# Reordering the first row group's second-layer products, two weight casts and three inverse roots

## The chip, the cores and the metric

The kernel runs on one core of one Trainium2 chip. The metric is the device time of one execution in microseconds (us). Three timed runs of the kernel before took 400.53, 398.08 and 399.92 us, median 399.92 us. Below, TensorE (PE) is the matrix engine, VectorE (DVE) and ScalarE (ACT) are the two elementwise engines that read its results, GpSimd (POOL) is the third elementwise engine, and SyncE (SP) issues the transfers.

## The reference

Each of 2048 rows of 512 numbers is normalised. The result is the input, plus a spectral filter of the normalised rows (a two-dimensional transform, a product with weights, the inverse transform), plus a two-layer network of the normalised rows:

```python
xn = _layernorm(x, axis=-1)              # x is 1 x 2048 x 512
X = rfft2(xn) * (w_r + 1j * w_i)         # spectral branch
y = irfft2(X, s=(S, D))
h = xn @ w1 + b1                         # w1 is 512 x 1792
act = h * tanh(softplus(h))              # "Mish"
return x + y + act @ w2                  # w2 is 1792 x 512
```

## The kernel before

Every product is made from 16-bit halves: a number is split into a high half (its 16-bit rounding) and a low half (what is left), and a product is three matmuls, high by high, high by low, low by high. The helper `mm3` (lines 85 to 92) issues these three for one output tile: line 88 takes both high halves, line 91 the high half of the stationary operand and the low half of the moving one, line 92 the reverse.

The 2048 rows are cut into four row groups of 512 (g = 0 to 3), and each into four blocks of 128 (s = 0 to 3). For each row group the network has 14 column tiles (f = 0 to 13). `mlp_up` makes one 128 x 512 tile of the first layer (12 matmuls, line 781, result `ph`); ScalarE applies Mish (line 795, tile `hb`) and makes its high half (line 813, tile `a`), VectorE the low half (line 816). `mlp_down(g, f, a)` adds the tile's part of the second layer into four accumulators `pa_0` to `pa_3`, one for each block of rows: 12 matmuls. Its moving operand is the weight `w2`, kept in seven pieces of two column tiles each, so tiles f = 2c and 2c + 1 read piece c. A piece is split by `hi_w2` on ScalarE (line 496) and `lo_w2` on VectorE (line 499); piece 0 is split earlier, by lines 379 and 380. Both halves lie in the tensor `w2r`.

After a start in which x, `w1` and `w2` are loaded and the first eleven up tiles are made, the program is written out in 26 slots, and within them PE, ACT, DVE and POOL keep the order in which the code is written (`in_order`). Each slot holds one up or down tile, and beside it pieces of the preparation of the later row groups: statistics of the rows (`sums_`, lines 209 and 211), the factors of the normalisation (`factors`, line 217 and on), the normalisation itself (`norm`: ScalarE lines 233 and 236, POOL line 237, tile `xh`), its transposition (`turned_rows`: PE line 242 into `pt`, then copies into `xnT` by VectorE line 333 and ScalarE line 334), and the first step of the spectral transform (`s1_forward`: PE into `psS`; ScalarE line 123 and VectorE lines 127 and 128 in `butterfly`, tiles `bc` and `bt`; ScalarE line 132 and POOL line 133 make `y`, which a transfer writes to memory). A piece of `w2` given to slot k is cast by ScalarE at the end of slot k and by VectorE in slot k + 1:

```python
for c in range(1, 7):
    at[(0, 3, 6, 8, 11, 14)[c - 1]]["w2"].append(c)
```

`factors` needs the inverse square root of a variance, 128 x 4 numbers for each row group. It is worked out by a bit trick and two polynomial steps. For row group 0 this is `rsqrt_of`, eight instructions on VectorE (lines 161 to 176) and a ninth for `nb`. For row groups 1 to 3 it is `rsqrt_plain`, eleven instructions on POOL (lines 187 to 197) and two for `nb` (lines 222 and 223).

The result tiles rotate through few buffers: `ph` and `pt` share two, the transform's `psS` and its successors two, `bt` two. A matmul into a tile waits until the tile two turns earlier has been read. After the slots come the rest of the spectral branch, with the up and down tiles of row groups 1 to 3 spread between its steps, and the outputs.

Of the kernel before, what the change touches and what calls it, by code (L numbers as in the profile page):

```python
# [12 lines left out]
F32 = mybir.dt.float32  # L13
I32 = mybir.dt.int32
AF = mybir.ActivationFunctionType
ALU = mybir.AluOpType
# [3 lines left out]
P = 128  # L20
# [21 lines left out]
def spectral_mlp_kernel(ctx, tc, x, wt, w0, w1, b1, w2, cT, cIT, cM, out):  # L42
    nc = tc.nc
# [3 lines left out]
    sp = ctx.enter_context(tc.tile_pool(name="sp", bufs=1))  # L47
# [38 lines left out]
    def mm3(ps, stat, mov, start, stop, order=False):  # L86

        first = nc.tensor.matmul(ps, stat(0), mov(0), start=start, stop=False)  # L88
        if order:
            tc.keep_in_program_order(first)  # L90
        nc.tensor.matmul(ps, stat(0), mov(1), start=False, stop=False)  # L91
        return nc.tensor.matmul(ps, stat(1), mov(0), start=False, stop=stop)  # L92
# [63 lines left out]
    def rsqrt_of(g, ve):  # L156

        r = sp.tile([P, 4], F32, tag="rr", name=f"rr_{g}_0", bufs=4)
        v = nc.vector

        v.tensor_scalar(r.bitcast(I32), ve.bitcast(I32), -0.5, float(0x5F3759DF), op0=ALU.mult, op1=ALU.add)
        t = sp.tile([P, 4], F32, tag="rt", name=f"rt_{g}_0", bufs=2)
        v.tensor_mul(t, r, r)
        q = sp.tile([P, 4], F32, tag="rq", name=f"rq_{g}_0", bufs=2)
        v.scalar_tensor_tensor(q, t, -192.0, ve, op0=ALU.mult, op1=ALU.mult)
        n = sp.tile([P, 4], F32, tag="rr", name=f"rr_{g}_1", bufs=4)
        v.scalar_tensor_tensor(n, q, 576.0, r, op0=ALU.add, op1=ALU.mult)

        t = sp.tile([P, 4], F32, tag="rt", name=f"rt_{g}_1", bufs=2)
        v.tensor_mul(t, n, n)  # L170
        w = sp.tile([P, 4], F32, tag="rq", name=f"rq_{g}_1", bufs=2)
        v.scalar_tensor_tensor(w, t, 384.0**-2, ve, op0=ALU.mult, op1=ALU.mult)
        p = sp.tile([P, 4], F32, tag="rt", name=f"rt_{g}_2", bufs=2)
        v.scalar_tensor_tensor(p, w, -10.0 / 3, w, op0=ALU.add, op1=ALU.mult)
        rs = sp.tile([P, 4], F32, tag="rs", name=f"rs_{g}", bufs=2)
        v.scalar_tensor_tensor(rs, p, 5.0, n, op0=ALU.add, op1=ALU.mult)
        return rs

    def rsqrt_plain(g, ve):


        def tile_(name):
            return sp.tile([P, 4], F32, tag=f"g{name}", name=f"g{name}_{g}", bufs=2)

        v = nc.gpsimd
        r, t, q, n, w, u, rs = (tile_(k) for k in ("r", "t", "q", "n", "w", "u", "s"))
        v.tensor_scalar(r.bitcast(I32), ve.bitcast(I32), -0.5, float(0x5F3759DF), op0=ALU.mult, op1=ALU.add)
        v.tensor_mul(t, r, r)
        v.tensor_mul(q, t, ve)
        v.tensor_scalar(q, q, -192.0, 576.0, op0=ALU.mult, op1=ALU.add)  # L190
        v.tensor_mul(n, q, r)
        v.tensor_mul(t, n, n)
        v.tensor_mul(w, t, ve)
        v.tensor_scalar(u, w, 384.0**-2, -10.0 / 3, op0=ALU.mult, op1=ALU.add)
        v.tensor_mul(u, u, w)
        v.tensor_scalar(u, u, 384.0**-2, 5.0, op0=ALU.mult, op1=ALU.add)
        v.tensor_mul(rs, u, n)
        return rs

    def sums(g, ts, ss):  # L200

        if 0 in ss:
# [11 lines left out]
    def factors(g, mv):  # L214

        ve = sp.tile([P, 4], F32, tag="ve", name=f"ve_{g}", bufs=2)
        nc.vector.tensor_scalar(ve, mv[:, :, 1], 1e-5, None, op0=ALU.add)
        nb = sp.tile([P, 4], F32, tag="nb", name=f"nb_{g}", bufs=2)
        if g:

            rs = rsqrt_plain(g, ve)
            nc.gpsimd.tensor_mul(nb, mv[:, :, 0], rs)
            nc.gpsimd.tensor_scalar(nb, nb, -1.0, None, op0=ALU.mult)
        else:
            rs = rsqrt_of(g, ve)
            nc.vector.scalar_tensor_tensor(nb, mv[:, :, 0], -1.0, rs, op0=ALU.mult, op1=ALU.mult)
        return mv, rs, nb

    def norm(g, s, ts, mr):
# [157 lines left out]
    w2t = w2r.rearrange("p c j d -> p c (j d)").bitcast(F16).rearrange("p c (h j d) -> p c h j d", h=2, j=2)  # L387
# [438 lines left out]
    pacc = {}  # L826

    def mlp_down(g, f, a):
        if f == 0:
            pacc[g] = [ps_a.tile([P, D], F32, tag="a", name=f"pa_{g}_{s}") for s in range(4)]  # L830
        for s in range(4):
            last_mm = mm3(
                pacc[g][s],
                lambda h: a[:, h, s * P : (s + 1) * P],
                lambda h: w2t[:, f // 2, h, f % 2, :],
                f == 0,
                f == NFC - 1,
            )
# [162 lines left out]
    xh, mr, mv = {(0, s): xhs[s] for s in range(4)}, {}, {}  # L1001
    at = {k: {"sums": [], "norm": [], "turn": [], "w2": [], "then": []} for k in range(N_SLOTS)}
# [26 lines left out]
    at[19]["then"].append(matrices)  # L1029
    at[21]["then"].append(load_it)  # L1030
    for c in range(1, 7):
        at[(0, 3, 6, 8, 11, 14)[c - 1]]["w2"].append(c)

    for k in range(N_SLOTS - 10, N_SLOTS):
        at[k]["then"].append(lambda: next(maxima, None))
# [2 lines left out]
    _, hi, lo = last["up"]  # L1038
# [44 lines left out]
    start, used = done[0], 0.0  # L1083
# [8 lines left out]
    start, n = done[0], len(todo)  # L1092
# [187 lines left out]
```

## Time and profile before

| what | before |
|---|---|
| median of three runs | 399.92 us (398.08 to 400.53) |
| the profiled execution's own time | 398.09 us |
| its span, first to last instruction | 396.3 us |
| PE busy | 379.8 us (96%) |
| VectorE busy | 241.2 us (61%) |
| ScalarE busy | 210.3 us (53%) |
| POOL busy | 68.9 us (17%) |
| transfers | 61.61 MB |
| granted PE clock | 1.00 |

A row of the timeline gives the start in us, the duration in us, the engine and the line of the kernel, the operation, the output and inputs by the program's names without their numbers, and the shapes; a bracket holds the idle time of that engine just before, and what released it. Consecutive instructions of an engine overlap a little, so a row's duration is longer than the distance to the next start.

### The profile page before, as it was taken

The page shows a single profiled execution, that of the slowest core. Times are in us where ns is not written, and L with a number is a line of the kernel's source. Part 1 is how long each engine was busy: PE and PEld are TensorE (multiplying, and loading weights), DVE is VectorE, ACT ScalarE, POOL GpSimd, SP SyncE. Part 2 cuts the span into 40 slices and gives each one's busy share as a digit, 9 for nine tenths or more (in the row PEclk, how much of TensorE's full clock was granted, in tenths as well). Part 3 has the DMA queues.
Part 4 walks back from the last instruction along what each step waited for, and adds up shares of the span by engine and source line. Part 5 has one row for each costly group of instructions (what it writes and reads, how often), then busy time and mean ns, then how long its engine had stood idle before and what let it go on. Part 6 is the DMA issues. An engine that isn't in the chain of part 4 may idle for free. (4 is left out here: it accounts for less than half of the span.)

```text
span 396.3 us, 6567 instructions
## 1 busy us (share of the span) xinstructions
PE 379.8 (96%) x2481; PEld 190.7 (48%) x2481; DVE 241.2 (61%) x505; ACT 210.3 (53%) x337; POOL 68.9 (17%) x100
## 2 busy tenths in 40 slices
PE   8799897999999999999999999999999999999995
PEld 3444343455544445456444565454655456444442
DVE  5789773465566724984597644957349972424334
ACT  3869858478665426564644555366455464423110
POOL 0000018366644400000021100121001120220000
PEclk9999999999999999999999999999999999999999
DMA  8995014335157894055732636226652022744556
GB/s 286 372 402 244 1 55 132 108 126 168 53 160 217 237 276 127 0 134 131 242 108 80 163 105 180 91 104 159 216 160 80 27 81 73 218 151 135 172 194 253
DMA packets 49519, 61.61 MB, mean 155 GB/s; under 512 B 3776, under 2 KB 36032, under 8 KB 48848
## 3 DMA queue, kind: packets, MB, share of 16 engines
q1 hardware_dynamic: 49488, 61.20, 49.1%
q8 instruction: 19, 0.31, 0.3%
q14 instruction: 12, 0.10, 0.1%
HBM read 44.38 MB, written 16.78 MB: 154 GB/s over the span
## 5 line engine op out<-in xcount | busy, mean ns | idle before, releaser
L781 PE MATMUL ph<-xnT,w1t 128*128 128x512 f16 x672 | 153.4, 379 | 1.3 <-ACT xnT L334 0.8
L781 PEld LDWEIGHTS <-w1t 128*128 128x128 f16 x672 | 65.0, 98 | 78.6 <-issue 1.5
L91 PE MATMUL pa<-w2r,a 128*128 128x512 f16 x224 | 84.9, 379 | 2.9 <-DVE w2r L499 1.9
L88 PE MATMUL pa<-w2r,a 128*128 128x512 f16 x224 | 85.0, 379 | 0.8 <-ACT w2r L496 0.5
L92 PE MATMUL pa<-w2r,a 128*128 128x512 f16 x224 | 84.9, 379 | 0.0
L795 ACT ACTIVATE hb<-ph,b1t,sc_exp 128x512 f32<-128x512 f32 x56 | 43.2, 772 | 56.1 <-PE ph L781 56.0
L816 DVE SCALAR_TENSOR_TENSOR a<-hb,sc_a,a 128x512 f16<-128x512 f32 x56 | 41.8, 750 | 51.0 <-ACT a L813 50.7
L133 POOL TENSOR_TENSOR tt<-bt_t,tt 128x512 f16<-128x512 f32 x16 | 19.9, 1245 | 186.3 <-ACT tt L132 186.3
L813 ACT ACTIVATE a<-hb,sc_a 128x512 f16<-128x512 f32 x56 | 40.1, 720 | 1.5
L92 PEld LDWEIGHTS <-a 128*128 128x128 f16 x224 | 21.9, 98 | 29.1 <-issue 3.7
L91 PEld LDWEIGHTS <-a 128*128 128x128 f16 x224 | 21.9, 98 | 25.5 <-issue 1.9
L88 PEld LDWEIGHTS <-a 128*128 128x128 f16 x224 | 21.9, 98 | 25.2 <-issue 0.8
L379 ACT ACTIVATE u<-r,sc_u 128x512 f16<-128x512 f32 x16 | 11.5, 720 | 23.6 <-DVE r L679 15.5
L133 POOL TENSOR_TENSOR y<-bt_s,y 128x512 f16<-128x512 f32 x16 | 18.7, 1177 | 10.8 <-issue 6.0
L132 ACT CAST tt<-bt_t 128x512 f16<-128x512 f32 x16 | 9.9, 616 | 15.9 <-DVE bt_t L128 12.5
L906 DVE SCALAR_TENSOR_TENSOR m<-psY,sc_k,m 128x512 f32<-128x512 f32 x12 | 8.7, 746 | 14.9 <-PE psY L92 14.9
L237 POOL TENSOR_TENSOR xh<-xs,xh 128x512 f16<-128x512 f32 x12 | 14.5, 1210 | 10.3 <-ACT xh L236 10.3
L734 DVE SCALAR_TENSOR_TENSOR at<-psA,at 128x512 f16<-128x512 f32 x16 | 10.7, 687 | 8.7 <-ACT at L733 8.7
L611 ACT ACTIVATE ix<-psD 64x512 f32<-64x512 f32 x16 | 9.5, 594 | 11.2 <-PE psD L599 10.9
L132 ACT CAST y<-bt_s 128x512 f16<-128x512 f32 x16 | 9.9, 616 | 10.4 <-DVE bt_s L128 7.6
L588 DVE SCALAR_TENSOR_TENSOR z<-psP,z 128x512 f16<-128x512 f32 x16 | 10.5, 684 | 7.8 <-ACT z L587 7.8
L127 DVE SCALAR_TENSOR_TENSOR bt_s<-psS,bc_s 128x256 f32<-128x256 f32 x16 | 6.7, 422 | 13.1 <-ACT bc_s L123 9.5
(158 smaller groups left out, 512.7 us busy)
## 6 DMA issues: line engine op xcount, KB each, us to landing
wt<-in_wt_dram SPq DMA_DIRECT2D x32, 256.0 KB
x<-in_x_dram SPq DMA_DIRECT2D x8, 512.0 KB
d_y<-y SPq DMA_DIRECT2D x16, 256.0 KB
wm<-in_wt_dram SPq DMA_DIRECT2D x8, 512.0 KB
yt<-d_y SPq DMA_DIRECT2D x16, 256.0 KB
d_a<-at SPq DMA_DIRECT2D x32, 128.0 KB
ai<-d_a SPq DMA_DIRECT2D x16, 256.0 KB
d_t<-tt SPq DMA_DIRECT2D x16, 256.0 KB
```

The source lines that it names most:

```text
L88: first = nc.tensor.matmul(ps, stat(0), mov(0), start=start, stop=False)
L91: nc.tensor.matmul(ps, stat(0), mov(1), start=False, stop=False)
L92: return nc.tensor.matmul(ps, stat(1), mov(0), start=False, stop=stop)
L132: nc.scalar.copy(out[:, :, 0, :], tv)
L133: nc.gpsimd.tensor_sub(out[:, :, 1, :], tv, out[:, :, 0, :])
L237: nc.gpsimd.tensor_sub(xh[:, 1, :], xs, xh[:, 0, :])
L379: hi = nc.scalar.activation(dst_h, src, AF.Copy, scale=scale)
L734: nc.vector.scalar_tensor_tensor(at[:, :, 1, :], psv, 2.0**-15, at[:, :, 0, :], op0=ALU.mult, op1=ALU.subtract)
L781: last_mm = nc.tensor.matmul(ph, w1t[:, hs, dc, f * P : (f + 1) * P], xnT[g][:, hm, dc, :], start=n == 0, stop=n == 11)
L795: nc.scalar.activation(hb, ph, AF.Mish, bias=b1t[:, f : f + 1], scale=s_exp[k])
L813: hi = nc.scalar.activation(a[:, 0, :], hb, AF.Copy, scale=sc["a"])
L816: lo = nc.vector.scalar_tensor_tensor(a[:, 1, :], hb, sc["a"], a[:, 0, :], op0=ALU.mult, op1=ALU.subtract)
```

## The change

Three things are done. In row group 0, a down tile with even f, which is the first of the two that read its piece of `w2`, issues its twelve matmuls in three passes over the four accumulators: four with both high halves, four with the low half of the activation and the high half of `w2`, and four with the low half of `w2`. Odd tiles, and all tiles of the other row groups, keep `mm3`. Pieces 2 and 3 of `w2` are given to slots 2 and 5 where they had slots 3 and 6. And the roots of row groups 1 to 3 are worked out by `rsqrt_of` on VectorE, so `rsqrt_plain` goes.

```diff
-    def rsqrt_plain(g, ve):
...
-        v = nc.gpsimd
-        r, t, q, n, w, u, rs = (tile_(k) for k in ("r", "t", "q", "n", "w", "u", "s"))
-        v.tensor_scalar(r.bitcast(I32), ve.bitcast(I32), -0.5, float(0x5F3759DF), op0=ALU.mult, op1=ALU.add)
...
-        v.tensor_mul(rs, u, n)
-        return rs
...
-        if g:
-
-            rs = rsqrt_plain(g, ve)
-            nc.gpsimd.tensor_mul(nb, mv[:, :, 0], rs)
-            nc.gpsimd.tensor_scalar(nb, nb, -1.0, None, op0=ALU.mult)
-        else:
-            rs = rsqrt_of(g, ve)
-            nc.vector.scalar_tensor_tensor(nb, mv[:, :, 0], -1.0, rs, op0=ALU.mult, op1=ALU.mult)
+        rs = rsqrt_of(g, ve)
+        nc.vector.scalar_tensor_tensor(nb, mv[:, :, 0], -1.0, rs, op0=ALU.mult, op1=ALU.mult)
...
     def mlp_down(g, f, a):
         if f == 0:
             pacc[g] = [ps_a.tile([P, D], F32, tag="a", name=f"pa_{g}_{s}") for s in range(4)]
+        rows = [slice(s * P, (s + 1) * P) for s in range(4)]
+        if g == 0 and f % 2 == 0:
+
+            for n, (ha, hw) in enumerate(((0, 0), (1, 0), (0, 1))):
+                for s in range(4):
+                    nc.tensor.matmul(
+                        pacc[g][s], a[:, ha, rows[s]], w2t[:, f // 2, hw, 0, :], start=f == n == 0, stop=False
+                    )
+            return
         for s in range(4):
-            last_mm = mm3(
+            mm3(
                 pacc[g][s],
-                lambda h: a[:, h, s * P : (s + 1) * P],
+                lambda h: a[:, h, rows[s]],
...
-        at[(0, 3, 6, 8, 11, 14)[c - 1]]["w2"].append(c)
+        at[(0, 2, 5, 8, 11, 14)[c - 1]]["w2"].append(c)
```

The changed file has fewer lines: up to its `mlp_down`, a line of it has a number 27 lower than before (ScalarE's cast of a piece is line 469 in place of 496, VectorE's 472 in place of 499, the low half of an activation 789 in place of 816). The new matmuls are line 809.

On PE, the start of the down tile f = 4 of row group 0 (activation `a_4_424`, first reader of piece 2 of `w2`, which lies in `w2r`), before:

```order
L88 LDWEIGHTS a_4_424
L88 MATMUL pa_0_557<-w2r,a_4_424 128x512
L91 LDWEIGHTS a_4_424
L91 MATMUL pa_0_557<-w2r,a_4_424 128x512
L92 LDWEIGHTS a_4_424
L92 MATMUL pa_0_557<-w2r,a_4_424 128x512
L88 LDWEIGHTS a_4_424
L88 MATMUL pa_1_558<-w2r,a_4_424 128x512
```

And the same place now:

```order
L809 LDWEIGHTS a_4_424
L809 MATMUL pa_0_557<-w2r,a_4_424 128x512
L809 LDWEIGHTS a_4_424
L809 MATMUL pa_1_558<-w2r,a_4_424 128x512
L809 LDWEIGHTS a_4_424
L809 MATMUL pa_2_559<-w2r,a_4_424 128x512
L809 LDWEIGHTS a_4_424
L809 MATMUL pa_3_560<-w2r,a_4_424 128x512
L809 LDWEIGHTS a_4_424
L809 MATMUL pa_0_557<-w2r,a_4_424 128x512
```

The second matmul of the tile read the low half of `w2` before; now the ninth is the first to do so.

On ScalarE, the rows from the cast of `y_1` in slot 2 on (`hb_11` is the Mish of up tile 11, `xs` and `xh` the first normalised block of row group 1, line 496 the cast of piece 2), before:

```order
L132 CAST y_1_650<-bt_s_1_653 128x4x128
L795 ACTIVATE hb_11_668<-ph_11_637,b1t,sc_exp_317 128x512
L813 ACTIVATE a_8_504<-hb_11_668,sc_a 128x512
L123 ACTIVATE bc_s_2_685<-psS_2_664 128x256
L233 ACTIVATE xs_691<-x_0_122,nb_609,gs_616 128x512
L236 CAST xh_690<-xs_691 128x512
L132 CAST y_2_684<-bt_s_2_687 128x4x128
L496 ACTIVATE w2r<-w2r,sc_w_515 128x1024
```

And now:

```order
L132 CAST y_1_647<-bt_s_1_650 128x4x128
L469 ACTIVATE w2r<-w2r,sc_w_515 128x1024
L768 ACTIVATE hb_11_666<-ph_11_634,b1t,sc_exp_317 128x512
L786 ACTIVATE a_8_504<-hb_11_666,sc_a 128x512
L123 ACTIVATE bc_s_2_683<-psS_2_662 128x256
L206 ACTIVATE xs_690<-x_0_122,nb_609,rs_624 128x512
L209 CAST xh_689<-xs_690 128x512
L132 CAST y_2_682<-bt_s_2_685 128x4x128
```

The cast of piece 2 moved from behind `y_2` to the place between `y_1` and the Mish of tile 11.

On VectorE, the rows of slots 2 and 3 (line 217 is the variance of row group 1, line 499 the low half of piece 2, `bt_s` the transform's tiles), before:

```order
L217 TENSOR_SCALAR ve_607<-mv_574 128x4
L127 SCALAR_TENSOR_TENSOR bt_s_1_653<-psS_1_633,bc_s_1_651 128x4x64
L128 SCALAR_TENSOR_TENSOR bt_s_1_653<-psS_1_633,bc_s_1_651 128x4x64
L816 SCALAR_TENSOR_TENSOR a_8_504<-hb_11_668,sc_a,a_8_504 128x512
L127 SCALAR_TENSOR_TENSOR bt_s_2_687<-psS_2_664,bc_s_2_685 128x4x64
L128 SCALAR_TENSOR_TENSOR bt_s_2_687<-psS_2_664,bc_s_2_685 128x4x64
L127 SCALAR_TENSOR_TENSOR bt_s_3_718<-psS_3_699,bc_s_3_716 128x4x64
L128 SCALAR_TENSOR_TENSOR bt_s_3_718<-psS_3_699,bc_s_3_716 128x4x64
L499 SCALAR_TENSOR_TENSOR w2r<-w2r,sc_w_515 128x1024
```

And now, from the last three of the root's nine instructions on, which follow the variance:

```order
L174 SCALAR_TENSOR_TENSOR rt_2_622<-rq_1_620 128x4
L176 SCALAR_TENSOR_TENSOR rs_624<-rt_2_622,rr_1_616 128x4
L199 SCALAR_TENSOR_TENSOR nb_609<-mv_574,rs_624 128x4
L127 SCALAR_TENSOR_TENSOR bt_s_1_650<-psS_1_630,bc_s_1_648 128x4x64
L128 SCALAR_TENSOR_TENSOR bt_s_1_650<-psS_1_630,bc_s_1_648 128x4x64
L789 SCALAR_TENSOR_TENSOR a_8_504<-hb_11_666,sc_a,a_8_504 128x512
L127 SCALAR_TENSOR_TENSOR bt_s_2_685<-psS_2_662,bc_s_2_683 128x4x64
L128 SCALAR_TENSOR_TENSOR bt_s_2_685<-psS_2_662,bc_s_2_683 128x4x64
L472 SCALAR_TENSOR_TENSOR w2r<-w2r,sc_w_515 128x1024
L127 SCALAR_TENSOR_TENSOR bt_s_3_716<-psS_3_697,bc_s_3_714 128x4x64
```

The root stands between the variance and `bt_s_1`, so `bt_s_1` and all behind it come after it; the low half of piece 2 moved ahead of `bt_s_3`.

More of the change, by code (lines that the diff above doesn't have):

```diff
@@ L177, in rsqrt_of @@
         return rs
-    def rsqrt_plain(g, ve):
-        def tile_(name):
-            return sp.tile([P, 4], F32, tag=f"g{name}", name=f"g{name}_{g}", bufs=2)
-        v = nc.gpsimd
-        r, t, q, n, w, u, rs = (tile_(k) for k in ("r", "t", "q", "n", "w", "u", "s"))
-        v.tensor_scalar(r.bitcast(I32), ve.bitcast(I32), -0.5, float(0x5F3759DF), op0=ALU.mult, op1=ALU.add)
[L188 to L196, printed above, removed]
-        v.tensor_mul(rs, u, n)
-        return rs
     def sums(g, ts, ss):
```

## The prediction

> **What bounds the kernel now.** I read the page first, then the waits of PE, then the timeline around each wait.
>
> ```profile
> span 396.3 us, 6567 instructions
> PE 379.8 (96%) x2481; PEld 190.7 (48%) x2481; DVE 241.2 (61%) x505; ACT 210.3 (53%) x337; POOL 68.9 (17%) x100
> PEclk9999999999999999999999999999999999999999
> ```
>
> PE is busy for 379.8 of 396.3 us at full granted clock, and no other engine is above 61%. The change neither adds nor removes a matmul, so all it can win is part of the 16.5 us in which PE stands still, and all it can lose is new standing still. The profiled execution took 398.09 us, 1.8 us around its span, and equals the fastest of the three timed runs; the median, 399.92 us, lies 1.83 us above it, and the timed runs spread over 2.45 us. I make the sum on the profiled execution and carry the difference to the median.
>
> The waits of PE (engine, tile and line, then who ended the wait: sum, times, longest):
>
> ```profile
> PE pa L91 <- DVE w2r L499: 1.9, 1, 1.9
> PE ph L781 <- ACT xnT L334: 0.8, 1, 0.8
> ```
>
> The longest single wait of PE is one of the second layer's matmuls for the low half of `w2`. The timeline shows it and its like, the only idle brackets of PE between 47 and 117 us:
>
> ```profile
> 47.27 0.38 PE L88 MATMUL pa<-w2r,a 128*128 128x512 f16 x1 [0.29 <-ACT w2r L379]
> 48.59 0.38 PE L91 MATMUL pa<-w2r,a 128*128 128x512 f16 x1 [0.94 <-DVE w2r L380]
> ...
> 60.67 0.38 PE L88 MATMUL psS<-xh,cTt 128*128 128x512 f16 x1
> ...
> 63.69 0.38 PE L92 MATMUL pa<-w2r,a 128*128 128x512 f16 x1
> 64.61 0.38 PE L88 MATMUL pa<-w2r,a 128*128 128x512 f16 x1 [0.54 <-ACT w2r L496]
> 66.93 0.38 PE L91 MATMUL pa<-w2r,a 128*128 128x512 f16 x1 [1.94 <-DVE w2r L499]
> ...
> 69.30 2.75 PE L781 MATMUL ph<-xnT,w1t 128*128 128x512 f16 x12
> ```
>
> From 66.93 to 69.30 eleven matmuls start, one each 0.2155 us. By that pitch the matmul of 48.59 was due at 47.49, so tile f = 0 lost 1.10 us to the low half of piece 0. The one of 64.61 was due at 63.91 and lost 0.70; the next was due 0.22 after it and lost 2.10. Tile f = 4 thus lost 2.80 us to piece 2. Pieces 1, 3, 4, 5 and 6 cost nothing: no bracket stands at their tiles. **3.90 us is all that the change can win here.** The 0.29 at 47.27 waits for piece 0's high half, which nothing in the change makes earlier.
>
> **The change, part by part.** *The three passes.* The halves of pieces 0 and 2 are made here:
>
> ```profile
> 47.25 1.28 DVE L380 SCALAR_TENSOR_TENSOR w2r<-w2r,sc_w 128x1024 f16<-128x1024 f32 x1 [1.15 <-ACT w2r L379]
> ...
> 65.61 1.27 DVE L499 SCALAR_TENSOR_TENSOR w2r<-w2r,sc_w 128x1024 f16<-128x1024 f32 x1
> ...
> 63.42 1.15 ACT L496 ACTIVATE w2r<-w2r,sc_w 128x1024 f16<-128x1024 f32 x1
> ```
>
> Eight matmuls now come before the first that reads a low half: 8 x 0.2155 = 1.72 us. For f = 0 that one is due at 47.27 + 1.72 = 48.99, and the low half was there for a matmul at 48.59. The wait goes: **1.10 us won**. The work between is matmuls that must run anyway, so the cover costs nothing. The passes also change the accumulator with each matmul. The row of 60.67 to 69.30 contains such changes (from `psS` to `pa`, and from one `pa` to the next after each third matmul) at the same pitch, so I price the order itself at zero; the rival below bounds it.
>
> *The earlier cast of piece 2, and the root in front of it.* In place of behind `y_2`, ScalarE casts piece 2 right behind `y_1`. But `y_1` waits for `bt_s_1` on VectorE, and there the root of row group 1 now comes first. Row group 0's root ran on VectorE in this profile, so its price is in the trace, from the variance to the next work that needs nothing of it:
>
> ```profile
> 7.04 0.17 DVE L217 TENSOR_SCALAR ve<-mv 128x4 f32<-128x4 f32 x1
> 7.24 0.17 DVE L161 TENSOR_SCALAR rr<-ve 128x4 int32<-128x4 int32 x1
> ...
> 8.82 0.16 DVE L226 SCALAR_TENSOR_TENSOR nb<-mv,rs 128x4 f32<-128x4 f32 x1
> 8.90 1.00 DVE L276 TENSOR_SCALAR xs<-x,mv,rs 128x512 f32<-128x512 f32 x2
> ```
>
> Nine instructions, 0.197 us apart, since each needs the one before; 8.90 - 7.04 = 1.86 us. The same distance now lies between the variance and `bt_s_1`, in place of 0.08:
>
> ```profile
> 56.57 0.17 DVE L217 TENSOR_SCALAR ve<-mv 128x4 f32<-128x4 f32 x1
> 56.65 0.42 DVE L127 SCALAR_TENSOR_TENSOR bt_s<-psS,bc_s 128x256 f32<-128x256 f32 x1
> 56.98 0.41 DVE L128 SCALAR_TENSOR_TENSOR bt_s<-psS,bc_s 128x256 f32<-128x256 f32 x1
> 59.51 0.75 DVE L816 SCALAR_TENSOR_TENSOR a<-hb,sc_a,a 128x512 f16<-128x512 f32 x1 [2.12 <-ACT a L813]
> 62.10 0.43 DVE L127 SCALAR_TENSOR_TENSOR bt_s<-psS,bc_s 128x256 f32<-128x256 f32 x1 [1.84 <-POOL y L133]
> ```
>
> ```profile
> 57.43 0.62 ACT L132 CAST y<-bt_s 128x512 f16<-128x512 f32 x1 [2.00 <-DVE bt_s L128]
> 57.95 0.77 ACT L795 ACTIVATE hb<-ph,b1t,sc_exp 128x512 f32<-128x512 f32 x1
> 58.76 0.72 ACT L813 ACTIVATE a<-hb,sc_a 128x512 f16<-128x512 f32 x1
> ...
> 62.89 0.62 ACT L132 CAST y<-bt_s 128x512 f16<-128x512 f32 x1 [0.46 <-DVE bt_s L128]
> ...
> 64.47 0.36 ACT L123 ACTIVATE bc_s<-psS 128x256 f32<-128x256 f32 x1
> ...
> 69.34 1.14 ACT L496 ACTIVATE w2r<-w2r,sc_w 128x1024 f16<-128x1024 f32 x1
> ```
>
> Up to the variance VectorE and ScalarE follow each other and not PE, so they stay where they are while PE is 1.10 ahead. Then: `bt_s_1` starts at 56.57 + 1.86 = 58.43, its second half at 58.76, and ends at 59.17. `y_1` starts 0.04 later (as at 57.43), 59.21; the cast of piece 2 0.52 behind it, 59.73; the Mish of tile 11 1.05 behind that (63.42 to 64.47), 60.78; its high half at 61.59, ending at 62.31, so VectorE's low half of tile 11 runs from 62.34 to 63.09; `bt_s_2` follows at 63.00 and 63.34. It also needs `bc_s_2`, which ScalarE makes right behind the high half, and POOL's `y_0` to be done, which it was by 62.10 even behind POOL's root; now no root stands ahead of it. The low half of piece 2 follows at 63.68 and ends at 64.95; a matmul can start 0.05 later, at 65.00.
>
> PE starts f = 4 at 63.91 - 1.10 = 62.81, with the high half long done (59.73 + 1.15 = 60.88). The ninth matmul is due at 62.81 + 1.72 = 64.53 and waits until 65.00, **0.47 us**. Four matmuls later, at 65.86, the next up tile starts, which started at 69.30. **The sum is 3.44 us won**, 1.10 of it at f = 0 and 2.34 at f = 4. The page "VectorE: DVE Perf Modes" of the Trainium skill gives in its errata section a table row of 58 cycles plus one for each element at 0.96 GHz for a VectorE instruction, an estimate of 65 ns for four elements; by it the root would add 0.6 us in place of 1.78, the 0.47 would be gone and the sum would be 3.90. The rows of the first root, 0.197 us apart, do not bear that out, and the same section says that about 150 cycles were measured.
>
> What queues behind the later `bt_s_1`: the buffer of its `psS` goes to the matmul of 60.67, due at 59.57 now, 0.35 us after the buffer is free at 59.22. I take no wait; were the root 0.5 us longer, PE would wait 0.15 us.
>
> *The earlier cast of piece 3.* It leaves VectorE's chain behind tile 12 and enters ScalarE's row before it. These four rows bear on it:
>
> ```profile
> 72.10 0.78 ACT L795 ACTIVATE hb<-ph,b1t,sc_exp 128x512 f32<-128x512 f32 x1 [1.61 <-PE ph L781]
> ...
> 75.17 1.28 DVE L499 SCALAR_TENSOR_TENSOR w2r<-w2r,sc_w 128x1024 f16<-128x1024 f32 x1
> ...
> 78.20 0.59 ACT L334 COPY xnT<-pt 128x512 f16<-128x512 f16 x1 [2.29 <-DVE xnT L333]
> ...
> 79.26 0.61 PE L242 MATMUL pt<-cMt,xh 128*128 128x128 f16 x8
> ```
>
> ScalarE ran from `y_2` at 62.89 to the end of piece 3's cast at about 70.39 without a gap and with two casts, 7.50 us; now one cast is in that stretch, 6.45 us, and `y_2` starts at 63.79 (end of `bt_s_2` at 63.75 and 0.04). So the Mish of tile 12 starts at 70.24; keeping its place behind PE it would be 72.10 - 3.44 = 68.66. It is 1.58 late. On VectorE the low half of piece 3, 1.19 us from start to next start, no longer stands between that Mish and the copy of 78.20: net 0.39 late. That copy frees the buffer of the transposition at 79.26, with 79.26 - 78.79 - 0.05 = 0.42 us to spare. I take zero and keep 0.4 us as the other end. Piece 3 itself was never late and wins nothing.
>
> *The other two roots.* Each puts 1.78 us on VectorE and takes thirteen instructions off POOL, where no matmul waited for them. Ahead of the copies they delay there is cover:
>
> ```profile
> 83.08 0.75 DVE L816 SCALAR_TENSOR_TENSOR a<-hb,sc_a,a 128x512 f16<-128x512 f32 x1 [1.22 <-ACT a L813]
> ...
> 86.22 0.59 ACT L334 COPY xnT<-pt 128x512 f16<-128x512 f16 x1 [0.86 <-DVE xnT L333]
> ...
> 89.22 2.75 PE L781 MATMUL ph<-xnT,w1t 128*128 128x512 f16 x12
> ```
>
> VectorE idled 1.22 us behind the second root's place, so 0.6 of its 1.78 comes through; the copy of 86.22 ended 2.4 us before the up tile that needs it. Cost zero; if the cover went, up to 1.78 each. From 112 us on, the wait of 0.8 at line 781 follows PE's own matmuls through VectorE and stays. I carry 3.44 us to the end: 398.09 - 3.44 = 394.65, and from the median 399.92 - 3.44 = 396.5 us.
>
> **The rivals.** *All of it is won*: the chain in slot 2 is 0.5 us shorter than I sum it, since a wait I put in serially overlaps. For it: I added each step at its full distance. Against: each is from a row. It gives 3.90, so 396.0 us.
>
> *Won and given back*: the burst of transfers before the spectral stage, and not PE, sets when that stage starts.
>
> ```profile
> 132.39 1.16 POOL L133 TENSOR_TENSOR y<-bt_s,y 128x512 f16<-128x512 f32 x1 [2.58 <-ACT y L132]
> ...
> 134.00:149.00 15.00, 15.00 (x88) 6.92 (x88) 4.79 (x10) 3.75 (x6) 2.68 (x8) 1.00 0.99 256
> ```
>
> In this stretch (the last two columns are the transfers' share and GB/s) the transfers are at 0.99. If they do not start sooner, PE meets them 3.44 us earlier and waits: 399.9 us, no change. Against it: the burst comes behind the last `y`, at 132.39, which waits for ScalarE, VectorE and in the end PE's own last `psS`, so it moves with PE.
>
> *Slower: the roots land on PE.* All three sit on VectorE ahead of copies that free the two buffers of `ph` and `pt`. If PE comes 3.44 us sooner and the copies do not, the distance of 2.4 us at 89.22 is used up once the copies fall 2.4 us back against PE: 1.78 for the root and 0.6 more. With every root in full on PE it is 3 x 1.78 = 5.34 lost against 3.90 won: 399.92 + 1.4 = 401.4 us. Against it stand the 1.22 idle above, and that PE had no bracket at all between 66.93 and 117 us.
>
> *The passes slow the matmuls.* The only slower matmuls in this profile are those at its start:
>
> ```profile
> 1.17 8.12 PE L251 MATMUL ps_warm<-warm 128*128 128x512 f16 x29 [1.17 <-DVE warm L246]
> ```
>
> Their pitch is (8.12 - 0.38) / 28 = 0.276 us. If all 84 matmuls of the seven even tiles ran so, that would be 84 x 0.061 = 5.1 us lost, 1.7 net: 401.6 us. The page "TensorE: Matmul & The Clock Gate" of the Trainium skill describes this in its section on a second failure mode, where cycling through PSUM banks leaves gaps and the clock gate falls back. The granted clock above is 9 in every slice, though three-matmul groups already cycle through four accumulators.
>
> **How the numbers follow.** About 1% of the time, 4 us, is what a measurement here can tell from no change. Forecast (3.0 to 3.7 won): 0.57. All won, or a little more: 0.20. Part lost to the margins of 0.35 and 0.42 us, 2 to 3 won: 0.12. Given back: 0.07. Roots on PE: 0.03. Slow matmuls: 0.01. The likeliest is 396.5 us. The range takes the win of 3.90 at its full, from the faster mode of the runs that the profiled execution shows (398.09 - 3.90 = 394.2), and reaches up to a win of 0.7, 399.2, which leaves out most of the last three cases. A win of 3.44 is 0.86%; medians of runs that spread over 2.45 us carry it past 1% in about four of ten cases of the forecast and in half of the second: faster 0.36, same 0.61, slower 0.03.
>
> **What would show it.** Right: the brackets of 0.94 and 0.54 are gone and 1.94 has become about 0.4 at line 809; the up tile of 69.30 starts near 65.9; the Mish of tile 11 comes after a cast of `w2`; the span is near 392.9 us. Wrong: a bracket of PE at a `pt` or `psS` between 59 and 100 us, a wait for `yt` near 145, a pitch above 0.2155 us at line 809, or a clock digit below 9.

## The result, and the profile after

| what | before | after |
|---|---|---|
| median of nine runs each | 398.94 us (398.07 to 400.53) | 395.84 us (395.00 to 398.49) |
| the profiled execution's own time | 398.09 us | 395.97 us |
| its span | 396.3 us | 394.2 us |
| PE's standing still (span less busy) | 16.5 us | 13.8 us |

The ratio after to before is 0.9917, 95% interval 0.9891 to 0.9943, so the kernel became 0.8% faster; the forecast was 396.5 / 399.92 = 0.9914. That the two ratios agree so closely is luck, as shown below: the span won 2.1 us where 3.44 were forecast, and the medians won 3.1. The difference is that 25 of 35 executions of the kernel before showed a granted clock of 0.994 to 0.996 and took 1.8 us longer than the ten at 1.000, and most of the changed kernel's did not (the last section has the numbers). So wins are read below in the traces first.

The head of the page of the changed kernel:

```profile
span 394.2 us, 6554 instructions
PE 380.4 (96%) x2481; PEld 191.0 (48%) x2481; DVE 246.2 (62%) x532; ACT 209.9 (53%) x337; POOL 59.9 (15%) x61
PEclk9999999999999999999999999999999999999999
```

PE has as many matmuls as before. VectorE gained 27 instructions (three roots of nine), POOL lost 39 (three of thirteen). The group of the new matmuls, on the same page (count, busy time, mean ns of one, idle time before them):

```profile
L809 PE MATMUL pa<-w2r,a 128*128 128x512 f16 x84 | 19.4, 379 | 0.6 <-DVE w2r L472 0.3
```

The 84 matmuls of the passes cost 0.6 us of idle time, and one takes 379 ns as any other 512-wide matmul does. PE's timeline at the two places that the sum was made for, and up to the third transposition of row group 1:

```profile
47.41 2.75 PE L809 MATMUL pa<-w2r,a 128*128 128x512 f16 x12 [0.29 <-ACT w2r L352]
...
59.71 0.38 PE L88 MATMUL psS<-xh,cTt 128*128 128x512 f16 x1
...
62.95 1.89 PE L809 MATMUL pa<-w2r,a 128*128 128x512 f16 x8
65.14 1.02 PE L809 MATMUL pa<-w2r,a 128*128 128x512 f16 x4 [0.30 <-DVE w2r L472]
66.00 2.75 PE L754 MATMUL ph<-xnT,w1t 128*128 128x512 f16 x12
...
73.37 2.75 PE L754 MATMUL ph<-xnT,w1t 128*128 128x512 f16 x12
76.27 0.61 PE L215 MATMUL pt<-cMt,xh 128*128 128x128 f16 x8
```

The whole trace lies 0.14 us later than that of before from its first tile of the second layer on (47.41 against 47.27). With that 0.14, the ninth matmul of f = 4 was forecast for 65.14 and the up tile behind it for 66.00, and that is where they stand: 3.44 us won, as summed. The loss at the ninth matmul is 65.14 - 62.95 - 8 x 0.2155 = 0.47 us, also as summed (the bracket counts from the modelled end of the row above, so it shows less). The last row is the first surprise. Twelve matmuls from 73.37 end their turn at 73.37 + 2.59 = 75.96, and the transposition starts at 76.27: 0.31 us lost, without a bracket.

What happened there stands in the timelines of ScalarE, VectorE and POOL of the changed kernel, in this order:

```profile
68.02 1.14 ACT L469 ACTIVATE w2r<-w2r,sc_w 128x1024 f16<-128x1024 f32 x1
...
70.42 0.77 ACT L768 ACTIVATE hb<-ph,b1t,sc_exp 128x512 f32<-128x512 f32 x1
...
75.63 0.59 ACT L307 COPY xnT<-pt 128x512 f16<-128x512 f16 x1 [1.10 <-DVE xnT L306]
```

```profile
62.48 0.75 DVE L789 SCALAR_TENSOR_TENSOR a<-hb,sc_a,a 128x512 f16<-128x512 f32 x1 [3.15 <-ACT a L786]
...
69.19 1.34 DVE L472 SCALAR_TENSOR_TENSOR w2r<-w2r,sc_w 128x1024 f16<-128x1024 f32 x1 [3.44 <-ACT w2r L469]
...
71.98 1.24 DVE L789 SCALAR_TENSOR_TENSOR a<-hb,sc_a,a 128x512 f16<-128x512 f32 x1 [1.11 <-ACT a L786]
73.14 0.41 DVE L127 SCALAR_TENSOR_TENSOR bt_s<-psS,bc_s 128x256 f32<-128x256 f32 x1
...
75.21 0.39 DVE L306 COPY xnT<-pt 128x512 f16<-128x512 f16 x1
```

```profile
69.41 3.26 POOL L210 TENSOR_TENSOR xh<-xs,xh 128x512 f16<-128x512 f32 x2
```

The same places in the trace of before, VectorE and then POOL:

```profile
73.66 0.75 DVE L816 SCALAR_TENSOR_TENSOR a<-hb,sc_a,a 128x512 f16<-128x512 f32 x1 [0.69 <-ACT a L813]
74.49 0.42 DVE L127 SCALAR_TENSOR_TENSOR bt_s<-psS,bc_s 128x256 f32<-128x256 f32 x1
```

```profile
68.97 2.28 POOL L237 TENSOR_TENSOR xh<-xs,xh 128x512 f16<-128x512 f32 x2
```

The Mish of tile 12 is at 70.42; 70.24 and the offset is 70.38. But the low half behind it took 1.24 us in place of 0.75, and POOL was in a two-input subtract until 72.67. So VectorE's next instruction starts 1.16 us behind the start of the low half (71.98 to 73.14), where it was 0.83 before (73.66 to 74.49): 0.33 us later. By the prediction's sum and the offset, ScalarE's copy was due at 78.20 - 3.44 + 0.39 + 0.14 = 75.29; it starts at 75.63, and the transposition that needs the buffer starts 0.05 behind its end.

POOL was still in its subtracts because the change put piece 3 beside them: the pair took 3.26 us in place of 2.28, and its first half started at 69.41, while VectorE was in the low half of piece 3 (69.19 to 70.53). The nine traces with piece 3 in slot 5 have 3.25 or 3.26 for this pair, the four with it in slot 6 have 2.27 or 2.28.

The other waits of PE, summed by tile (sum, times, longest):

```profile
PE psT L88 <- DMA ai<-d_a: 2.3, 3, 1.3
...
PE ph L754 <- ACT xnT L307: 0.8, 1, 0.8
...
PE pa L809 <- DVE w2r L472: 0.3, 1, 0.3
```

The wait for `ai` near 193 us, and the same one in the trace of before:

```profile
192.79 0.20 PE L88 MATMUL psT<-ai,cMt 128*128 128x64 f16 x1 [1.34 <-DMA ai<-d_a]
```

```profile
195.25 0.20 PE L88 MATMUL psT<-ai,cMt 128*128 128x64 f16 x1 [0.80 <-DMA ai<-d_a]
```

The 0.8 at the up tile near 114 us stayed, as forecast. The wait for the transfer of `ai` was 0.80 and is 1.34 here. So the 3.44 came down to 3.13 at the transposition, 2.61 behind the transfer of `ai`, and 2.24 at the end of the span; less the 0.14 of the start that is 396.3 - 394.2 = 2.1.

### The profile page after: what moved, and what is told of

Its sections match the earlier page's. It is cut to its first block, busy times and chain, and to the rows that moved or that the text cites. A ratio compares the mean times of both kernels' runs of the same rounds, so it can differ in the third digit from the quotient of the medians.

```text
span 394.2 us, 6554 instructions
## 1 busy us (share of the span) xinstructions
PE 380.4 (96%) x2481; PEld 191.0 (48%) x2481; DVE 246.2 (62%) x532; ACT 209.9 (53%) x337; POOL 59.9 (15%) x61
## 5 line engine op out<-in xcount | busy, mean ns | idle before, releaser
L88 PE MATMUL pa<-w2r,a 128*128 128x512 f16 x196 | 74.4, 380 | 0.0
L91 PE MATMUL pa<-w2r,a 128*128 128x512 f16 x196 | 74.3, 379 | 0.0
L92 PE MATMUL pa<-w2r,a 128*128 128x512 f16 x196 | 74.3, 379 | 0.0
L92 PEld LDWEIGHTS <-a 128*128 128x128 f16 x196 | 19.2, 98 | 22.5 <-issue 0.2
L88 PEld LDWEIGHTS <-a 128*128 128x128 f16 x196 | 19.2, 98 | 21.8 <-issue 0.8
L91 PEld LDWEIGHTS <-a 128*128 128x128 f16 x196 | 19.2, 98 | 21.0 <-issue 0.5
L809 PE MATMUL pa<-w2r,a 128*128 128x512 f16 x84 | 19.4, 379 | 0.6 <-DVE w2r L472 0.3
L210 POOL TENSOR_TENSOR xh<-xs,xh 128x512 f16<-128x512 f32 x12 | 15.7, 1311 | 18.5 <-ACT xh L209 18.2
```

Source lines behind the costliest of these rows:

```text
L210: nc.gpsimd.tensor_sub(xh[:, 1, :], xs, xh[:, 0, :])
L809: nc.tensor.matmul(pacc[g][s], a[:, ha, rows[s]], w2t[:, f // 2, hw, 0, :], start=f == n == 0, stop=False)
```

## The experiments

The theory was that of the prediction with one addition: the win is the waits for `w2` and no more; VectorE's chain in slot 2, with the root in it, sets what is left at f = 4; and what is lost behind that goes to the copies ahead of the third transposition. The rivals: that the win adds up from independent parts, that the roots' place on VectorE is harmless, and that the loss behind 70 us comes from elsewhere.

For each kernel three numbers are given: its ratio to the kernel before with its 95% interval, and from the traces how far ahead of before it is at the up tile behind f = 4 and at the end of its span, with the offset of its own start taken off (up tile: 69.30 in the trace of before; end: 396.3).

### The passes alone

The kernel before with the three passes:

```diff
+        if g == 0 and f % 2 == 0:
+            for n, (ha, hw) in enumerate(((0, 0), (1, 0), (0, 1))):
+                for s in range(4):
+                    nc.tensor.matmul(...)
+            return
```

> Only the three passes; pieces of w2 and roots as before. Theory (each half of a piece is released by a chain of ScalarE and VectorE that does not follow PE): the 0.94 us wait at f = 0 goes and PE is 1.10 us ahead, but piece 2's high half is still ready only at about 64.6, so f = 4 starts where it did, its first wait grows to 1.6 us, the ninth matmul waits about 0.6 for the low half, and the up tile that started at 69.30 starts near 67.8: 1.5 us won, not 1.10 + 2.10. Rival (each wait for a low half is hidden by itself): 3.2 us won, the up tile near 66.1.

Measured: 396.75 us, ratio 0.9939 [0.9913, 0.9965]; 1.51 us ahead at the up tile and 1.79 at the end. PE's timeline:

```profile
47.36 2.75 PE L836 MATMUL pa<-w2r,a 128*128 128x512 f16 x12 [0.28 <-ACT w2r L379]
...
64.70 1.89 PE L836 MATMUL pa<-w2r,a 128*128 128x512 f16 x8 [1.64 <-ACT w2r L496]
67.02 1.02 PE L836 MATMUL pa<-w2r,a 128*128 128x512 f16 x4 [0.43 <-DVE w2r L499]
67.88 2.75 PE L781 MATMUL ph<-xnT,w1t 128*128 128x512 f16 x12
```

The wait at f = 0 is gone, 1.10 won, and PE then waits 1.64 us for the cast of piece 2, where it waited 0.54: the high half comes at the same time as before, and PE is merely there sooner. What the passes win in all is 69.30 - 67.88 + 0.09 = 1.51, set by f = 4 alone. By the same rows f = 0 could have been left as it was: the cast of piece 2 hangs on ScalarE's and VectorE's chain and not on PE, so 1.51 should have come out all the same. That is an argument from the rows; no run leaves f = 0 alone.

### The earlier pieces alone

```diff
-        at[(0, 3, 6, 8, 11, 14)[c - 1]]["w2"].append(c)
+        at[(0, 2, 5, 8, 11, 14)[c - 1]]["w2"].append(c)
```

> Only pieces 2 and 3 one slot sooner; matmuls in the old order, roots on POOL. Theory: the wait of 0.94 us at f = 0 stays; with no root on VectorE ahead of y_1 the cast of piece 2 starts near 58.0 and its low half ends near 64.1, just as the second matmul of f = 4 is due (64.13): both waits there go, 2.8 us won. Rival (casting earlier only moves the delay to the Mish and the low half behind it): the low half ends near 65, 0.9 us of wait stays, 1.9 us won.

Measured: 396.06 us, ratio 0.9915 [0.9886, 0.9944]; 2.62 ahead at the up tile, 2.91 at the end. PE shows the old wait of 0.94 at f = 0 and no bracket at f = 4, though its second matmul there is 0.18 late, which is what is missing to the 2.80 that f = 4 lost before: two steps of VectorE's chain take longer than in the trace of before. (The end is further ahead than the up tile mainly because the wait for `ai` was only 0.37 in this execution.) VectorE's timeline:

```profile
60.56 1.60 DVE L816 SCALAR_TENSOR_TENSOR a<-hb,sc_a,a 128x512 f16<-128x512 f32 x1 [3.15 <-ACT a L813]
62.08 0.41 DVE L127 SCALAR_TENSOR_TENSOR bt_s<-psS,bc_s 128x256 f32<-128x256 f32 x1
...
62.75 1.51 DVE L499 SCALAR_TENSOR_TENSOR w2r<-w2r,sc_w 128x1024 f16<-128x1024 f32 x1
```

and POOL's beside it:

```profile
60.45 2.73 POOL L133 TENSOR_TENSOR y<-bt_s,y 128x512 f16<-128x512 f32 x2
63.15 2.14 POOL L237 TENSOR_TENSOR xh<-xs,xh 128x512 f16<-128x512 f32 x1
```

VectorE's low half of tile 11 took 1.60 in place of 0.75 under POOL's `y`, and the low half of piece 2 took 1.51 in place of 1.27. This kernel has the roots on POOL, and they push `y` into these instructions; the changed kernel, with the roots on VectorE, has `y` out of the way and pays for the root instead.

### The roots alone

```diff
-        if g:
-            rs = rsqrt_plain(g, ve)
...
+        rs = rsqrt_of(g, ve)
+        nc.vector.scalar_tensor_tensor(nb, mv[:, :, 0], -1.0, rs, op0=ALU.mult, op1=ALU.mult)
```

> Only the roots of row groups 1 to 3 on VectorE. Theory: y_1 starts 1.8 us later, but ScalarE no longer waits 1.2 us for POOL's factors, so piece 2 is cast at 63.3 as before (63.42): both waits at f = 4 stay within 0.2 us, nothing won or lost, 0.0 to 0.2 us. Rival 1 (the root lands on PE): up to 1.8 us lost at each row group. Rival 2 (POOL's relief is worth time): 0.5 us or more won.

Measured: 399.08 us in ten runs, ratio 0.9995 [0.9976, 1.0014]; 0.10 ahead at the up tile, 0.05 behind at 117 us, 0.53 behind at the end. In the slots the roots alone neither win nor cost anything that can be told: the waits at f = 4 are still there (0.43 and 1.94 by PE's brackets), and behind the first root the order of before leaves time, since there piece 2 comes only behind `y_2`. The 0.5 at the end is lost behind 215 us, and the medians at one clock (last section) show it too, though the ratio does not.

### The passes and the pieces, with the roots on POOL

The first two edits together, `factors` as before.

> The changed kernel with the roots of row groups 1 to 3 back on POOL. Theory (the root on VectorE delays y_1, and with it the cast, the Mish and the low half): no wait at f = 4, the up tile near 65.4 us, 3.9 us won there; y_2 near 62.9, so the copy ahead of the third transposition of row group 1 is in time and the 0.3 us before that transposition goes too; in all 0.5 to 0.8 us better than the changed kernel. Rival (the roots belong to the win, since POOL's root holds the normalisation and its small instructions slow VectorE): the same as the changed kernel or up to 1 us worse.

Measured: 394.38 us, ratio 0.9879 [0.9848, 0.9909]; 3.90 ahead at the up tile, 3.68 at the end. PE's timeline:

```profile
47.35 2.75 PE L836 MATMUL pa<-w2r,a 128*128 128x512 f16 x12 [0.29 <-ACT w2r L379]
...
62.89 2.75 PE L836 MATMUL pa<-w2r,a 128*128 128x512 f16 x12
65.48 2.75 PE L781 MATMUL ph<-xnT,w1t 128*128 128x512 f16 x12
...
113.69 2.75 PE L781 MATMUL ph<-xnT,w1t 128*128 128x512 f16 x12 [0.78 <-ACT xnT L334]
```

All 3.90 us that the prediction named as the most that can be won are won, and f = 4 runs without a wait. VectorE's low half of tile 11 again takes 1.59 us here, but ScalarE's `y_1` is at 57.51 in place of 59.35, and the 1.84 us buy more than the 0.84 that POOL costs. The parts alone were worth 1.51 and 2.62, together 4.13: they overlap by 0.23, since only 3.90 were there, so the rival that they simply add up is off by little. Of the three parts, then, two make the win and the third gives part of it back. The third transposition loses only 0.08 us here (72.84 + 2.59 = 75.43, and it starts at 75.51), although POOL stretches the low half of tile 12 to 1.53 us: ScalarE's Mish of that tile is at 69.37 and not at 70.42. So the stretched low half alone does not cost the 0.31; it does behind the late Mish. No run has the late Mish alone; by the sum, 0.03 us of the margin would have been left with it.

### Which of the roots costs

Two kernels, the passes and the pieces in both: one with only row group 1's root on POOL, one with only row group 1's on VectorE.

```diff
-        if g:
+        if g == 1:
```

> The changed kernel with only row group 1's root back on POOL; the roots of row groups 2 and 3 on VectorE. Theory (the first root alone costs PE in the slots, 0.5 us at f = 4 and 0.3 before the transposition): no wait at either place, up tile near 65.4, at most 0.2 us lost between 70 and 112 us; time within 0.3 us of the kernel with all roots on POOL. Rival (each root on VectorE costs by itself, or the wait for ai near 192 us grows with any root on VectorE): 0.7 us or more behind that kernel.

```diff
-        if g:
+        if g > 1:
```

> The reverse: only row group 1's root on VectorE, ahead of y_1 as in the changed kernel; groups 2 and 3 on POOL. Theory: both waits stay as in the changed kernel (0.3 us bracket at f = 4, 0.3 before the transposition), 0.8 us behind the kernel with all roots on POOL up to 112 us, and the time that of the changed kernel within 0.3. Rival: most of the cost was in groups 2 and 3, time near that of POOL's roots.

Measured: with root 1 on POOL 394.85 us, ratio 0.9901 [0.9870, 0.9933], 3.90 ahead at the up tile, 3.56 at the end; with root 1 on VectorE 395.88 us, ratio 0.9918 [0.9891, 0.9945], 3.44 and 3.17. The second has the same row at f = 4 as the changed kernel:

```profile
65.07 1.02 PE L836 MATMUL pa<-w2r,a 128*128 128x512 f16 x4 [0.31 <-DVE w2r L499]
65.93 1.24 PE L781 MATMUL ph<-xnT,w1t 128*128 128x512 f16 x5
```

The first root carries the loss at f = 4 and at the third transposition (3.13 ahead behind it, as in the changed kernel). The roots of groups 2 and 3 cost nothing up to 117 us (3.83 ahead there, against 3.84 with all three on POOL); what they cost behind that is at most the 0.5 or so between 394.85 and the two medians with all on POOL (394.38, and 394.30 below), and the intervals of these ratios overlap.

### The roots' cost, measured twice

The kernel with passes and pieces and the roots on POOL, and the changed kernel, both again unchanged, side by side:

> The kernel with the passes, the earlier pieces and all roots on POOL once more, beside the others on one chip. If the wait for ai near 192 us belongs to where the roots run, it is again clearly shorter than in the changed kernel (0.70 against 1.34 us); if it varies from execution to execution, the two overlap. Time 1.0 to 1.5 us below the changed kernel by the first theory, 0.7 by the second.

> The changed kernel once more, beside the others on one chip: waits of 0.3 us at f = 4 and 0.3 us before the transposition again, since both follow from the order; the wait for ai near 192 us again 1.2 us or more if it belongs to the roots, anywhere between 0.3 and 1.4 if it varies.

Measured: 394.30 us, ratio 0.9882 [0.9859, 0.9906], 3.91 ahead at the up tile, 3.97 at the end; and 395.76 us, ratio 0.9920 [0.9894, 0.9946], 3.43 and 2.85. So the roots on VectorE cost 1.46 us by the medians and 1.12 by the two traces. Of it 0.48 is lost at f = 4 (3.91 against 3.43 ahead) and 0.23 more up to 117 us (3.84 against 3.13), at the third transposition; 0.7 in the slots together. The rest is 0.4 us by the traces, lost in waits for transfers (0.14 at `ai` near 192 us, 0.23 at `yi` near 352), and 0.7 by the medians, and that is not settled: the wait for `ai` was 0.70 and 0.41 with the roots on POOL, and 1.34 and 0.55 with them on VectorE, two executions of the same kernel each. PE's wait at that place is 0.29 to 0.80 us in the six traces with all roots on POOL and 0.55 to 1.34 in the five with all on VectorE: longer on the whole, but the two overlap, and no run shows why.

### The root one slot later

The changed kernel, with `factors` behind the sums of the next slot, so that `y_1` doesn't wait for it:

```diff
-        if 3 in ss:
-            mr[g] = factors(g, mv[g])
...
+        at[a + 2]["root"].append(g)
...
+                for g in do["root"]:
+                    mr[g] = factors(g, mv[g])
```

> The changed kernel with each of the three roots one slot later, still on VectorE: behind bt_s_1 (and its likes bt_s_6 and bt_s_12's slot) in place of ahead of it. Theory (what the roots cost is their place ahead of y_1, not the engine): y_1 near 57.5, the cast of piece 2 near 58.0, the root in VectorE's idle time behind bt_s_1, the low half of piece 2 done near 63.3; no wait at f = 4, the up tile near 65.4, none before the third transposition, time equal to the kernel with POOL's roots within 0.3 us, so 0.7 us better than the changed kernel. Rival (nine small instructions on VectorE cost their 1.8 us wherever they stand): the 0.3 at f = 4 and the 0.3 before the transposition stay, time as the changed kernel.

Measured: 395.70 us, ratio 0.9895 [0.9861, 0.9929]; 3.91 ahead at the up tile, 3.57 at 117 us, 2.94 at the end. Both waits that the theory named are gone: f = 4 runs through (63.74, then the up tile at 66.33, 0.94 of it start offset), and PE loses nothing ahead of the third transposition. The low half of tile 12 is stretched here too, to 1.23 us, but the Mish ahead of it is in time. But the total is that of the changed kernel within the spread, and not 0.7 us better as expected. PE waits at a place that was free:

```profile
113.11 0.61 PE L215 MATMUL pt<-cMt,xh 128*128 128x128 f16 x8 [0.28 <-ACT hb L768]
114.82 2.75 PE L754 MATMUL ph<-xnT,w1t 128*128 128x512 f16 x12 [0.45 <-ACT xnT L307]
```

By the starts, 0.15 us goes between 92 and 109 us without a bracket, and 0.52 at the transposition of 113.11, of which the bracket shows 0.28. The up tile behind it regains 0.33, since it waits 0.45 where it waited 0.78 before. That makes the 0.34 lost up to there; 0.6 more goes behind 117 us, a third of it at the wait near 192 us. The theory was right on the two waits and too hopeful on the sum. The page of this execution shows one thing more, the granted clock in slice 2:

```profile
PEclk9899999999999999999999999999999999999999
```

Most of its offset of 0.94 us arises there. Six of the matmuls that run at the start take 2.77 us, and 1.46 in the trace of before, and the first up tile behind them starts at 18.60 in place of 17.66:

```profile
12.88 2.77 PE L224 MATMUL ps_warm<-warm 128*128 128x512 f16 x6
```

```profile
12.59 1.46 PE L251 MATMUL ps_warm<-warm 128*128 128x512 f16 x6
```

### Piece 3 where it was

The changed kernel with piece 3 back in slot 6:

```diff
-        at[(0, 2, 5, 8, 11, 14)[c - 1]]["w2"].append(c)
+        at[(0, 2, 6, 8, 11, 14)[c - 1]]["w2"].append(c)
```

> The changed kernel with piece 3 back in slot 6 (piece 2 stays in slot 2). Theory (moving piece 3 wins nothing at its own matmuls, but its low half on VectorE stands ahead of the copy that frees the buffer of row group 1's third transposition): that transposition waits 0.3 + 1.2 = 1.5 us, and the kernel is 1.2 us worse than the changed one. Rival (the prediction's own words: piece 3 wins nothing): 0.3 us as in the changed kernel, same time.

Measured: 396.91 us in eight runs, ratio 0.9931 [0.9910, 0.9952]; 3.43 ahead at the up tile as in the changed kernel, but 1.89 at 117 us and 0.68 at the end. PE's wait and VectorE's rows ahead of it:

```profile
77.45 0.61 PE L215 MATMUL pt<-cMt,xh 128*128 128x128 f16 x8 [1.38 <-ACT xnT L307]
```

```profile
72.29 0.75 DVE L789 SCALAR_TENSOR_TENSOR a<-hb,sc_a,a 128x512 f16<-128x512 f32 x1 [2.67 <-ACT a L786]
...
73.79 1.27 DVE L472 SCALAR_TENSOR_TENSOR w2r<-w2r,sc_w 128x1024 f16<-128x1024 f32 x1
74.98 1.28 DVE L188 BATCH_NORM_STATS2 st<-x 128x6 f32<-128x512 f32 x2
...
76.39 0.39 DVE L306 COPY xnT<-pt 128x512 f16<-128x512 f16 x1
```

The low half of piece 3 stands ahead of the copy for 1.19 us (73.79 to 74.98), the copy starts 1.18 later than in the changed kernel, and the transposition loses 1.5 in place of 0.3. The low half of tile 12 is back at 0.75 us, since POOL is done with its subtracts before it starts:

```profile
69.36 2.27 POOL L210 TENSOR_TENSOR xh<-xs,xh 128x512 f16<-128x512 f32 x2
```

That saves 0.34 us here (0.82 in place of 1.16 to the next start), and the Mish, at 70.74, takes about as much back. Piece 3 itself is late for nobody here; it is in the way of the copy.

### Copies ahead of the output additions

The passes and the pieces with the roots on POOL, and one edit that attacks the wait of 0.78 near 114 us. There VectorE makes the four additions that end row group 0 (`mlp_end`) ahead of the copy that the up tile waits for; they are held until the slot's copies and low halves are issued:

```diff
     def mlp_end(g):
+        if "held" in sc:
+            sc["held"].append(g)
+            return
...
+            sc["held"] = []
...
+            for g in sc.pop("held"):
+                mlp_end(g)
```

> The kernel with the passes and the earlier pieces and POOL's roots, and beside it row group 0's four additions into m (line 852 of the kernel before) behind the copy of the transposition and the low half of the slot, in place of ahead of them. Theory: the wait of 0.78 us of the up tile near 114 us goes, since the copy needs only the transposition, which is done some 3 us before that; 0.9 us better than that kernel, about 393.5 us. Rival (the additions, now later, hold the accumulators or bt_s_12, and a later wait takes the place): no change, 394.4 us.

Measured: 393.84 us (393.37 to 394.01), ratio 0.9854 [0.9823, 0.9885], in five runs; 4.79 ahead at the end, where the same kernel without this edit was 3.68 and 3.97 ahead. The wait of 0.78 is gone, and one that was 0.30 is 0.62:

```profile
122.41 0.61 PE L242 MATMUL pt<-cMt,xh 128*128 128x128 f16 x8 [0.62 <-ACT xnT L334]
```

So 0.3 of the 0.8 are given back at a later transposition; by the starts 0.6 is left there (4.45 us ahead against 3.84). By the medians this edit won 0.5 us (393.84 against 394.38 and 394.30) where 0.9 were expected. It is the best of the kernels here, ahead of both the kernel before and the changed one.

## Why the prediction was right or wrong

- **That only the waits for `w2` can be won, 3.90 us at most:** right in the slots. The kernel with the roots on POOL won 3.90 there, and none more.
- **The passes (1.10 won at f = 0, their order free):** right, with the 0.29 ahead of the first matmul staying as said. The rival of slower matmuls is out: twelve of them still take 2.75 us as an up tile's twelve do, and the clock is at 9 in all 40 slices, in the changed kernel and with the passes alone. What the Trainium skill's page "TensorE: Matmul & The Clock Gate" describes in its section on a second failure mode, with cycling through PSUM banks, did not show at this cycle of four, in which PE had no idle time between the matmuls of a pass.
- **Piece 2 and the root in front of it (0.47 left at the ninth matmul):** right to the hundredth, 0.47 measured. `y_1` was forecast for 59.21 and came at 59.35, the Mish of tile 11 for 60.78 and came at 60.93, the end of the low half for 64.95 and came at 65.09: each 0.14 or 0.15 late, the offset of the start. The variance and the nine instructions of the root take 56.71 to 58.58, about 0.197 us from start to start. The table row of 58 cycles in the errata section of the Trainium skill's page "VectorE: DVE Perf Modes" does not price a chain in which each needs the one before.
- **No wait at the `psS` behind `bt_s_1` (margin 0.35):** right; 59.71 is 12 matmuls of 0.2155 behind 57.12.
- **Piece 3 (took 0, other end 0.4):** the step that failed. The working had the copy 0.39 late against a margin of 0.42, which was right as far as it went. It took VectorE's low half of tile 12 at its old 0.75 us and left POOL out: the earlier piece 3 held up POOL's subtract, this stretched the low half, and the copy came 0.34 later still. With 0.03 us left of the margin, 0.31 was lost, and the other end, 0.4, was the nearer one. The sign that the prediction named for this, a bracket at a `pt`, would not have shown it, since the profile prints none there. "Piece 3 itself was never late and wins nothing" holds for its own matmuls; the 1.19 us that the working took off for it on VectorE is what the run with piece 3 back in slot 6 lost, 1.2 us.
- **The other two roots (zero):** right up to 117 us; behind that at most 0.5, not separated.
- **The wait of 0.8 near 117 us stays:** right (0.78).
- **The sum carried to the end (3.44, span 392.9):** wrong by 1.3 us in the first trace (394.2) and by 0.6 in the second (393.5). In the first, 0.3 of it is the transposition, 0.1 the start, and 0.9 lies in waits for `ai` and its like behind 190 us, which change from one execution to the next; the prediction had no term for a spread there.
- **The median (396.5):** 395.84 came out, inside the range, but the way to it was not that of the prediction. It subtracted 3.44 from a median that lay 1.83 above the profiled execution and kept that distance. The win in the spans was smaller (2.1 to 2.8), and the distance vanished too: the changed kernel's profiled execution, 395.97, lies at its median, 395.84. The kernel before itself came out at 398.94 in nine executions, and not at 399.92. These are errors of opposite sign, so the closeness of 0.9917 to 0.9914 is luck; the 3.44 in the slots is not.
- **The rivals:** all won (3.90) did not happen, but for a reason that the prediction had: the root. Given back at the burst of transfers did not happen: the changed kernel is 3.14 us ahead behind it (177.93 against 180.93, with the offset of 0.14 taken off) and ahead to the end. The roots did land on PE, by 0.7 us in the slots and not by 5.34.

## What to carry to other kernels

An operation that waits on an in-order engine is priced by who stands behind it on that engine: moving piece 3 won nothing for its own reader and 1.2 us at the copy that it no longer blocked, and a root moved to the engine that does it in half the time (1.87 us, against 3.6 on POOL, 56.92 to 60.52 in the first trace with the passes, the pieces and POOL's roots) cost 0.7 us in the slots because `y` and a cast queued behind it. When a margin comes out within some hundredths of a microsecond of zero, carry half of the other end, and look what the other engines do in that stretch. And test the parts of a change apart: here two parts won 3.9 us and the third took 0.7 of it back in the slots.

## What the runs showed of the hardware that was not expected

**VectorE and POOL slow each other.** With POOL in a two-input operation, VectorE's two-input low half of 128 x 512 numbers took 1.24, 1.59 and 1.60 us in place of 0.75, and the split of 128 x 1024 took 1.51 in place of 1.27; POOL's subtract took 2.14 beside it in place of the 1.16 that it takes alone. The halves of `bt_s`, which read one operand from `psS`, stayed at 0.41 beside the same POOL work. In the 13 traces, between 32 and 129 us, 190 low halves of 128 x 512 with no such POOL operation beside them took 0.74 or 0.75 us; the 14 that overlapped one by 0.68 us or more took 1.23 to 1.60. Of the two, the one that starts second pays: every low half and every split that took longer had started while POOL's operation ran. Where VectorE started first it kept its time and POOL's operation took 1.42 to 1.97 us in place of 1.16; in the changed kernel the split at 63.81 took 1.28 and the subtract that started at 64.14 took 1.96. Even a small instruction pays: in the kernel with the root one slot later, one on 128 x 4 numbers, 0.16 us alone, lasted to the end of POOL's `y`:

```profile
59.03 1.01 DVE L170 TENSOR_TENSOR rt<-rr 128x4 f32<-128x4 f32 x1
```

```profile
58.85 1.17 POOL L133 TENSOR_TENSOR y<-bt_s,y 128x512 f16<-128x512 f32 x1 [1.76 <-ACT y L132]
```

In the Trainium skill, the page "GPSIMD Engine Reference" says in its section on key points that POOL shares its SBUF interfaces with VectorE, with contention where VectorE has two SBUF inputs; the traces agree, and they add the size and the order. With the root on POOL, `y` was pushed into VectorE's work; that part of the cost the roots' move did take away.

**The granted clock changes between executions of one kernel.** Of 35 executions of the kernel before beside the experiments, ten show a mean granted clock of 1.000 and take 398.05 to 398.45 us, and 25 show 0.994 to 0.996 and take 398.49 to 401.10, median 400.03. That is 1.8 us, as large as the effects studied. Of 66 executions of the changed kernel and the experiments, 15 show 0.996 or less; whether the changes have a part in that is open. Taken at a clock of 0.998 and more alone, the medians give the wins that the traces gave, to within 0.7 us (the starts' offsets taken off in the traces):

| kernel | won by median at clock 0.998 and more | won at the end of the span, trace |
|---|---|---|
| the passes alone | 1.5 | 1.79 |
| the pieces alone | 2.2 | 2.91 |
| the roots alone | -0.5 | -0.53 |
| passes and pieces, roots on POOL, twice | 4.0, 3.9 | 3.68, 3.97 |
| the same, root 1 on VectorE | 3.2 (one execution) | 3.17 |
| the same, roots 2 and 3 on VectorE | 3.4 | 3.56 |
| the changed kernel, twice | 2.5, 2.7 | 2.24, 2.85 |
| the root one slot later | 2.7 | 2.94 |
| piece 3 where it was | 1.3 | 0.68 |
| copies first | 4.4 | 4.79 |

(The median of before at that clock is 398.24.) What lowers the clock was not tried; in the one profile that caught it, it falls in slice 2, 10 to 20 us into the span.
